# Twelve output stores of an attention and Fourier kernel, each in four pieces of 32 rows

## The chip, the cores and the metric

The kernel runs on one core of a Trainium2 chip. The metric is the device time of one execution in microseconds (us); lower is better. The engines are TensorE (PE; PEld are its weight loads), VectorE (DVE), ScalarE (ACT), GpSimd (POOL) and SyncE (SP), which here only issues transfers. ACT issues a few transfers too.

## The reference

The input is one sequence of 2048 tokens of 640 numbers in bf16. Two branches are mixed by a gate per token:

```
g = sigmoid((x * gate_w).sum(-1, keepdims=True))
a = attention(x, wq, wk, wv, wo, beta)      # 32 heads of 20, 4 segments of 512 tokens
b = irfft2(rfft2(B_x) * (w_r + 1j*w_i))     # over tokens and features
return g * a + (1 - g) * b
```

In each segment the attention is causal softmax attention within the segment. It is mixed per head, with sigmoid(beta), with a read of a memory: with phi(t) = t + 1 for positive t and exp(t) elsewhere, the read is phi(q) M / (phi(q) z + 1e-6). After a segment M and z grow by phi(k)^T v and by the sum of phi(k). The heads' outputs are then multiplied by wo. The first segment has an empty memory.

## The kernel before

The program is recorded as a list of operations with the buffers that each reads and writes, and then laid out by `Sched.schedule` (L111) in an order written out by hand as a list of numbers, `ORDER`. A number v stands for operation v // 2, on its first or second possible engine. Each engine runs its operations strictly in this order. `Sched.emit` (L249) puts in the waits: an operation waits for the last writer of what it reads and for the last users of what it overwrites.

A transfer is made by `Kern.dma` (L548 for a copy, L546 for a transposing load). Each gets one of 56 semaphores in turn and waits for the transfer that had the semaphore before; the bytes in flight are held under 1.6 MB. Nearly all transfers are issued by SP, one after another: an SP instruction that waits holds all that stand behind it.

Projections, attention and the Fourier transform fill PE through most of the program, interleaved. The end of a token's way is `finish_tile(s, a)` (L1506), for segment s and part a of it (four parts of 128 tokens):

- For the first three segments (s < 3) the attention's numerators come transposed from memory into `oU` (five loads, ld_u) and are multiplied by the reciprocal denominators `r4` (L1526, "normal"). The denominators go by way of memory: `rc` is stored into r_scr and loaded back as `r`.
- From the second segment on, the memory's part is loaded by a transposing load from o_scr into one of three buffers `mT`, and added to `oU` (L1534, "addmem").
- For each half of 320 columns PE sums in one PSUM bank the Fourier branch's last step ("Fb", L514, from `G` and the gate table `fbg`) and five products with wo ("oproj", L512). One copy to bf16, on ACT (L523) or DVE (L525), puts the half into one of four buffers `ot`.
- Then the finished 128 rows of 640 numbers, 160 KB, are stored from `ot`.

A row p = 32 q + j of `ot` holds token 512 s + 4 a + q + 16 j, so the four groups of 32 partitions are four token phases q. In the output these rows are 16 tokens apart. For s < 3 one transfer, st_out, stores the whole tile; its destination has the dimensions 4 phases, 32 tokens, 640 numbers. For the last segment (s = 3) four transfers, st_part, store a phase each, two issued by SP and two by ACT. The tile that reuses the `ot` buffer, four tiles later, waits until the stores out of it have landed.

In SP's order the first three st_out stand among the last loads of the third segment: after the store of `rc`; then come a key load `qkp` and a transposing load of `mT`; then the load of `r`; then two st_out; then two transposing loads of `mT`. The other nine stand behind these, the last eight with nothing but stores after them. At the very end SP waits for the semaphores of all output stores (L693), two to an instruction.

Of the kernel before, what the change touches and what calls it, by code (L numbers as in the profile page):

```python
# [12 lines left out]
P = 128  # L13
S = 2048
D = 640
# [3 lines left out]
L = 512  # L19
# [415 lines left out]
def dap(ap, off, *dims):  # L435
    return bass.AP(tensor=ap.tensor, offset=ap.offset + off, ap=[list(q) for q in dims])
# [25 lines left out]
class Kern:  # L462
# [10 lines left out]
    def b(self, *key):  # L473
        v = self.bufs.get(key)
        if v is None:
            v = self.bufs[key] = Buf(str(key))
        return v
# [64 lines left out]
    def dma(self, dst, src, nbytes, r, w, prio, tr=False, name="", after=(), queue="sp"):  # L542
# [16 lines left out]
        "ld_wka": (520.0, 1100.0, 16), "ld_wkb": (450.0, 2200.0, 16), "ld_wqa": (500.0, 1100.0, 16), "ld_wqb": (500.0, 2200.0, 16),  # L559
        "ld_wo": (600.0, 700.0, 16), "ld_wo2": (600.0, 3000.0, 16), "ld_wv": (450.0, 3000.0, 16), "ld_x": (450.0, 950.0, 16),  # L560
        "oT": (1300.0, 750.0, 16), "pad2": (370.0, 350.0, 10), "pad": (400.0, 1250.0, 10), ("pkT", 131072): (1260.0, 600.0, 16), ("pkT", 262144): (1280.0, 1100.0, 16),
        ("st_qk", 65536): (450.0, 220.0, 16), ("st_qk", 131072): (480.0, 350.0, 16), ("st_qk", 262144): (480.0, 720.0, 16), "st_g": (430.0, 150.0, 4), "st_o": (660.0, 950.0, 8), "st_out": (560.0, 1900.0, 4),
        "st_part": (430.0, 250.0, 16), "st_r": (480.0, 200.0, 16), "st_u": (520.0, 700.0, 16), ("xT", 131072): (1240.0, 1300.0, 16), ("xT", 262144): (1700.0, 2300.0, 16),
        ("xT", 393216): (1400.0, 2600.0, 16), ("xT", 655360): (2950.0, 2100.0, 16)}

    TSTART, TEND, F_START, F_END = 22.39, 193.27, 27.86, 215.71
# [75 lines left out]
        1564, 3542, 3072, 3544, 3129, 3088, 1568, 3546, 1603, 1570, 4012, 1529, 3122, 1573, 3138, 3432, 3148, 3125, 3548, 3552, 3194, 3150, 3564,  # L642
        3554, 1604, 3556, 3130, 3558, 3550, 3560, 1606, 3416, 1612, 3436, 3566, 3568, 3562, 3570, 1614, 3572, 3172, 3152, 3574, 3614, 3576, 3174,
        3438, 3578, 1608, 3580, 3440, 2562, 3442, 3583, 3444, 3196, 1574, 3616, 3446, 3618, 4034, 1577, 1610, 3156, 3176, 3620, 4016, 3622, 3158,
        1634, 3154, 4102, 3606, 3624, 1636, 3626, 1638, 3178, 3628, 3448, 3198, 3608, 3166, 1641, 1642, 3430, 3200, 1652, 3610, 3168, 1616, 1618,
        3612, 4030, 1620, 1644, 3170, 1654, 1623, 1646, 4028, 3654, 1656, 1648, 3160, 3184, 4042, 3584, 3656, 1658, 1650, 3162, 3670, 3250, 3658,
        3587, 1688, 3146, 3660, 3672, 1690, 2940, 1692, 3164, 3187, 1624, 1670, 1626, 4046, 1628, 4019, 1695, 3180, 2564, 1630, 3674, 1696, 1632,
        1698, 3182, 1700, 3214, 3202, 1702, 1660, 3216, 1678, 3188, 1672, 4036, 1680, 1674, 1662, 1704, 3462, 1664, 1682, 1676, 3588, 1666, 3206,
        3218, 4038, 1742, 1684, 3204, 3208, 1750, 4020, 1744, 1668, 1746, 3224, 1686, 3220, 1724, 1752, 1726, 4044, 1754, 1728, 1796, 3591, 3226,
        1748, 3230, 3222, 1730, 3598, 1756, 3232, 3464, 1798, 3210, 1800, 3600, 1732, 1758, 4080, 1734, 3228, 1736, 3602, 3238, 1803, 3470, 3212,  # L650
        3604, 3630, 1738, 3240, 3706, 3234, 3632, 3638, 1740, 3708, 1706, 3236, 3634, 1708, 3646, 3636, 1710, 4049, 4086, 3640, 3648, 3242, 1713,
        3710, 4090, 3650, 3642, 1778, 4023, 3652, 1780, 3244, 3688, 3644, 1714, 3690, 1716, 3246, 1782, 1804, 1718, 1806, 3692, 3694, 4024, 1808,
        1720, 1760, 3714, 4082, 1784, 1810, 3662, 4089, 1722, 4094, 1850, 3664, 1812, 3592, 1852, 1854, 3594, 1786, 3696, 3248, 1788, 1762, 1790,
        4040, 1858, 1860, 4222, 1862, 4032, 1764, 1856, 4092, 3748, 1766, 1792, 3678, 4206, 3750, 4208, 1864, 3666, 4210, 4098, 4212, 4214, 1794,
        1768, 3676, 4510, 1770, 1866, 1772, 4216, 4026, 4050, 3596, 4064, 4052, 4054, 4218, 3466, 3680, 1774, 3752, 1832, 4158, 3682, 1834, 3700,
        1836, 1776, 4056, 4066, 3754, 4068, 3252, 4070, 4072, 4058, 4150, 3668, 1840, 1842, 4074, 4154, 1838, 4084, 3756, 4076, 3698, 4146, 1844,
        3758, 3716, 1814, 1846, 1816, 4142, 3702, 3718, 3720, 3684, 1848, 4138, 3722, 3254, 3760, 4060, 4100, 3256, 4192, 4194, 3724, 3686, 4196,
        3726, 4062, 3774, 4096, 1818, 4078, 3776, 1886, 3728, 3762, 4198, 4200, 1820, 3468, 4202, 4104, 1888, 3778, 1822, 1824, 4224, 1826, 1890,
        3766, 3786, 1828, 4354, 4226, 3764, 1893, 3768, 4228, 4230, 3780, 1830, 4106, 4108, 4205, 4110, 3788, 4112, 4136, 4114, 4240, 3782, 4242,
        4116, 4220, 4232, 3790, 4234, 4119, 3792, 3784, 3802, 3794, 3804, 1894, 1896, 3704, 1898, 3806, 1900, 3808, 3770, 3796, 4244, 3772, 3810,  # L660
        4236, 1902, 4246, 4248, 4250, 4238, 3812, 3798, 3852, 3814, 4120, 3854, 4253, 3800, 4122, 4124, 1876, 4148, 4254, 3818, 3820, 4156, 1868,
        3822, 4140, 4256, 1870, 1872, 4144, 3824, 1874, 4152, 3928, 3712, 3826, 3732, 3828, 3930, 1878, 1880, 3734, 3736, 3830, 4160, 3856, 4320,
        3738, 4357, 4176, 3932, 3740, 4126, 4178, 3742, 4128, 4130, 3744, 4180, 4486, 3860, 4132, 4182, 3730, 3862, 1882, 3747, 4184, 4134, 4274,
        4358, 4360, 4362, 3864, 4186, 4258, 4364, 4366, 4368, 4189, 3866, 4418, 3920, 4370, 1884, 3858, 4490, 3922, 4276, 4322, 4260, 4372, 4262,
        3868, 4374, 4452, 4376, 4378, 4380, 4264, 4278, 4382, 4280, 4492, 4266, 3924, 4385, 3834, 4282, 3934, 3836, 4268, 4324, 4270, 4326, 3833,
        4162, 4273, 4328, 4284, 4330, 4164, 4287, 4166, 3870, 4168, 4332, 4170, 4288, 4334, 3816, 3842, 3838, 4336, 4402, 3844, 4404, 3872, 4406,
        4172, 4408, 3936, 4388, 4175, 4338, 4340, 3874, 4390, 4342, 4190, 4290, 3846, 4420, 4292, 4294, 4410, 3840, 4344, 4346, 4348, 3878, 3848,
        4351, 4296, 3880, 4392, 4412, 4352, 3850, 4394, 4298, 4415, 3888, 3876, 3890, 3892, 3894, 3882, 3884, 4304, 3896, 4396, 4300, 3898, 3886,
        4398, 4306, 4302, 4308, 3938, 4454, 4400, 3904, 4488, 3940, 3906, 4416, 3908, 3910, 3900, 3926, 4310, 4312, 3912, 4314, 4456, 3914, 4458,
        4317, 4470, 4472, 3942, 3946, 3916, 4318, 4460, 3948, 4436, 3902, 4474, 3944, 4462, 4464, 4438, 3950, 4466, 4440, 3952, 4442, 4469, 4476,  # L670
        4444, 3958, 4478, 4422, 3964, 3954, 3974, 3960, 3966, 4480, 4424, 4426, 3956, 4483, 4428, 4446, 4430, 4432, 4484, 3962, 3976, 3968, 3978,
        4435, 4386, 3970, 3980, 4448, 4498, 3972, 3982, 4494, 3984, 3990, 4450, 3992, 4496, 3986, 3994, 3996, 4500, 3989, 4548, 3998, 4526, 4512,
        4000, 4620, 3919, 4514, 4002, 4528, 4634, 4516, 4622, 4004, 4636, 4502, 4506, 4504, 4518, 4509, 4550, 4638, 4530, 4640, 4642, 4532, 4644,
        4552, 4534, 4647, 4520, 4624, 4522, 4536, 4626, 4525, 4628, 4538, 4562, 4564, 4566, 4568, 4546, 4540, 4630, 4570, 4554, 4633, 4542, 4544,
        4598, 4556, 4600, 4572, 4654, 4648, 4602, 4604, 4575, 4558, 4650, 4652, 4606, 4584, 4561, 4608, 4586, 4588, 4611, 4590, 4582, 4576, 4592,
        4594, 4578, 4580, 4597, 4614, 4616, 4618, 4612,
    )

    def texp(self, s, g, u=None):

# [3 lines left out]
    def build(self):  # L684
        nc = self.nc
        with nc.Block() as block:
            @block.gpsimd
            def _(pool):
                self.alloc()
                self.record()  # L690
                self.Sc.schedule(self.POOLS, self.ORDER)
                for s_, c in self.Sc.emit("st_out", "st_part"):
                    nc.sync.wait_ge(s_, c)  # L693

    def alloc(self):
# [810 lines left out]
    def finish_tile(self, s, a):  # L1506

        self.Sc.group += 1
        b = self.b
        prio = max(self.F_END + self.O_BASE + self.O_STEP * a, self.texp(s, 7, 4) + 4.0) if s < 3 else self.TEND + self.FIN[0] + self.FIN[1] * a  # L1510
        self.finc = getattr(self, "finc", -1) + 1
        k4 = self.finc % 4
        ot = self.ot[k4]
# [26 lines left out]
        otb = [b("ot", k4, hf) for hf in range(2)]  # L1540
        for hf in range(2):
# [14 lines left out]
            for c in range(5):  # L1556
# [5 lines left out]
                else:  # L1562
                    items = []
                    for q in range(4):
# [5 lines left out]
                self.mms(items, [b("oTl", c), b("wo2"), bank] if s == 3 else [ob[c], b("wo", c), bank], [], prio, name="oproj", mode=2 if s == 3 else -1)  # L1570
            self.Sc.op(self.copy_alts(lambda hf=hf: ot.ap(hf * 320, [1, 320]), lambda bank=bank: self.ps(bank, 0, [1, 320]), 320),
                       r=[bank], w=[otb[hf]], prio=prio, after=self.after_mid(("ot", k4, hf)), name="final")
        if s < 3:
            self.dma(lambda: dap(self.out, (s * L + 4 * a) * D, [D, 4], [16 * D, 32], [1, D]), lambda: ot.ap(0, [1, D]), P * D * 2, otb,
                     [b("out", s, a)], prio, name="st_out")
            return
        for q in range(4):
            self.dma(lambda q=q: dap(self.out, (s * L + 4 * a + q) * D, [16 * D, 32], [1, D]), lambda q=q: ot.ap(0, [1, D], p0=32 * q, np_=32),
                     32 * D * 2, otb, [b("out", s, a, q)], prio, name="st_part", queue=("sp", "act", "sp", "act")[q])

# [1 line left out]
_INS = ['A_x', 'A_wq', 'A_wk', 'A_wv', 'A_wo', 'A_beta', 'B_x', 'B_w_r', 'B_w_i', 'gate_w']  # L1582
# [24 lines left out]
```

## Time and profile before

| | |
|---|---|
| runs | 243.44, 241.42, 241.70 us; median 241.7 |
| profiled execution, its span (the page has no other time for it) | 245.4 us |
| PE, DVE, ACT, POOL busy | 228.8, 195.6, 199.9, 166.4 us |
| mean granted PE clock | 0.986 |
| output stores, 160 KB, from SP | 12 |
| output stores, 40 KB, from SP and from ACT | 8 and 8; 1.8 and 1.9 us to landing (median) |
| transposing loads of mT | 8; 5.5 us to landing (median) |
| SP's longest wait for a transfer after 180 us | 3.8 us, for r_scr |

The busy times are sums over the span and overlap. A transfer's time to landing runs from the start of its issue on SP to the last step of its semaphore. Times within the span count from its start.

### The profile page before, as it was taken

What the parts mean: (1) busy time and instruction counts of PE and PEld (TensorE: products, weight loads), DVE (VectorE), ACT (ScalarE), POOL (GpSimd) and SP (SyncE); (2) the same over time, 40 slices, a digit from 0 to 9 for tenths busy, and PEclk for the clock granted to TensorE, in tenths of its full rate; (3) what the DMA queues carried; (4) which work ended last, traced back from release to release, by engine and by line L of the source; (5) the groups of instructions that cost most, each with busy time, mean ns of one, the idle gap of its engine ahead of it and who ended that gap; (6) DMA issues with size and microseconds to landing.
All of it is one profiled execution on the core that took longest, in us unless ns stands there. A gap on an engine that the chain in (4) does not pass through costs nothing.

```text
span 245.4 us, 10243 instructions
## 1 busy us (share of the span) xinstructions
PE 228.8 (93%) x4347; PEld 140.8 (57%) x4361; DVE 195.6 (80%) x481; ACT 199.9 (81%) x241; POOL 166.4 (68%) x297
## 2 busy tenths in 40 slices
PE   7899999999999999999899999899999997699994
PEld 2574567765455665545556555465454565366794
DVE  0479998889999987989999898989889867435563
ACT  2289698988999999999899889999999976388740
POOL 8513268557969846768947998859898694359730
PEclk9999999999999999999999999999999999589999
DMA  7999959975799875575698661375758997812123
GB/s 168 278 365 208 239 160 178 318 140 164 210 200 174 168 226 143 125 199 135 202 233 234 185 186 53 99 210 146 222 151 194 230 140 96 127 36 85 57 84 108
DMA packets 58928, 42.17 MB, mean 172 GB/s; under 512 B 30020, under 2 KB 55172, under 8 KB 58884
## 3 DMA queue, kind: packets, MB, share of 16 engines
q1 hardware_dynamic: 57844, 40.96, 69.2%
q8 instruction: 34, 0.56, 1.0%
q10 hardware_dynamic: 1040, 0.57, 0.8%
q14 instruction: 10, 0.08, 0.1%
HBM read 23.32 MB, written 12.30 MB: 145 GB/s over the span
## 4 chain that ended last, share of the span: by engine, by line
PE 54%; DVE 18%; ACT 12%; DMA 10%; issue 3%; SPq 1%; DVEq 0%
PE psum L514 48%; ACT ex L1263 9%; PE psum L512 6%; DMA pkn<-phk 4%; DMA r_scr<-rc 3%; DMA xT<-in_A_x_dram 2%; DVE xsb L906 2%; DVE Pt L1439 2%; DVE xf L901 1%; DVE phk L1085 1%; ACT et L1072 1%; DVE oU L1526 1%; DVE G L1485 1%; DVE ub L525 1%; DVE va L1115 1%
## 5 line engine op out<-in xcount | busy, mean ns | idle before, releaser
L1263 ACT ACTIVATE ex<-psum 128x2048 bf16<-128x2048 f32 (+4 forms) x92 | 138.7, 1507 | 16.3 <-PE psum L514 14.3
L1284 POOL TENSOR_SCALAR_AFFINE_SELECT ex<-ex 128x256 bf16<-128x256 bf16 (+2 forms) x224 | 122.1, 567 | 42.0 <-ACT ex L1263 38.4
L514 PE MATMUL psum<-qkp 20*64 20x64 bf16 (+5 forms) x1280 | 32.7, 271 | 4.8 <-issue 2.3
L514 PE MATMUL psum<-xT,wk 128*128 128x256 bf16 (+1 forms) x280 | 34.0, 273 | 0.9 <-DMA wk<-in_A_wk_dram 0.6
L514 PE MATMUL psum<-wv,xT 128*32 128x321 bf16 (+3 forms) x400 | 30.0, 301 | 0.6 <-DVE va L1115 0.3
L514 PE MATMUL psum<-xT,wq 128*128 128x512 bf16 (+1 forms) x121 | 27.0, 380 | 1.3 <-DMA xT<-in_A_x_dram 0.7
L1439 DVE TENSOR_TENSOR Pt<-psum,Wt 128x642 bf16<-128x642 f32 x32 | 25.5, 820 | 2.3 <-PE psum L514 1.9
L514 PEld LDWEIGHTS psum<-qkp 20*64 20x64 bf16 x1280 | 13.4, 103 | 19.5 <-ACT ex L1263 13.2
L514 PEld LDWEIGHTS psum<-xT,wk 128*128 128x128 bf16 (+1 forms) x280 | 19.9, 97 | 7.0 <-DMA wk<-in_A_wk_dram 1.1
L512 PE MATMUL psum<-wo,oU 128*32 128x320 bf16 x480 | 23.4, 313 | 0.5 <-DVE oU L1534 0.5
L906 POOL TENSOR_TENSOR xsb<-xf 128x320 bf16<-128x320 bf16 (+2 forms) x12 | 9.2, 763 | 17.1 <-DVE xsb L906 13.2
L525 DVE CAST ot<-psum 128x320 bf16<-128x320 f32 x21 | 10.1, 491 | 12.9 <-PE psum L512 10.5
L514 PEld LDWEIGHTS psum<-wv,xT 128*32 128x32 bf16 (+1 forms) x400 | 14.3, 96 | 8.3 <-issue 2.4
L514 PE MATMUL psum<-big,Ac 128*128 128x160 bf16 (+2 forms) x96 | 18.1, 258 | 0.7 <-DVE Pt L1439 0.3
L1115 DVE TENSOR_TENSOR va<-psum,ebx 128x320 bf16<-128x320 f32 x32 | 15.2, 483 | 4.2 <-ACT gate L1113 2.1
L514 PE MATMUL psum<-big,Cp 128*128 128x321 bf16 (+1 forms) x96 | 18.0, 302 | 0.2 <-DVE G L1485 0.2
L514 PE MATMUL psum<-ex,va 128*32 128x64 bf16 (+3 forms) x576 | 17.4, 256 | 0.7 <-DVE dn L1152 0.3
L1485 DVE TENSOR_TENSOR G<-eo,psum 128x320 bf16<-128x320 f32 x32 | 14.7, 482 | 3.9 <-PE psum L514 2.8
L512 PEld LDWEIGHTS psum<-wo,oU 128*32 128x32 bf16 x480 | 12.4, 100 | 8.8 <-issue 4.2
L514 PE MATMUL psum<-tt,Yt 128*128 128x256 bf16 (+1 forms) x96 | 16.5, 275 | 0.3
L514 PEld LDWEIGHTS psum<-ex,va 128*32 128x32 bf16 x576 | 11.1, 96 | 9.7 <-POOL ex L1284 3.4
L1072 ACT ACTIVATE et<-qu 128x512 bf16<-128x512 bf16 x25 | 15.6, 630 | 0.2
(99 smaller groups left out, 391.9 us busy)
## 6 DMA issues: line engine op xcount, KB each, us to landing
qkp<-qk_scr SPq DMA_DIRECT2D x28, 160.0 KB
tt<-tab_tt SPq DMA_DIRECT2D x8, 512.0 KB, 4.3
qk_scr<-qu SPq DMA_DIRECT2D x12, 256.0 KB, 3.1
u_scr<-ub SPq DMA_DIRECT2D x12, 256.0 KB, 3.9
xsb<-in_A_x_dram SPq DMA_DIRECT2D x8, 320.0 KB, 6.8
oU<-u_scr SPq DMA_DIRECT2D x15, 128.0 KB, 2.9
out_dram<-ot SPq DMA_DIRECT2D x12, 160.0 KB
Wt<-in_B_w_r_dram SPq DMA_DIRECT2D x16, 80.2 KB, 2.6
```

The source lines that it names most:

```text
L512: h = e.matmul(dst, wt, r_, start=st, stop=sp_, **{**kw, "tile_position": (0, q), "skip_group_check": True})
L514: h = e.matmul(o_, l_, r_, start=st, stop=sp_, **kw)
L525: alts["dve"] = (lambda e: e.tensor_copy(dst(), src()), 67 + 1.04 * n, 68.0)
L901: self.either(lambda e, r=r, op=op: e.tensor_tensor(xf.ap(r * 642, [321, 2], [1, 320]), xs.ap(o, [D, 2], [1, 320]), xs.ap(o + 320, [D, 2], ...
L906: self.either(lambda e, dst=dst, src=src, d0=d0, n=n, op=op: e.tensor_tensor(xs.ap(o + dst, [D, 2], [1, n]), xf.ap(src + d0, [321, 2], [1, ...
L1072: self.one("act", lambda e: e.activation(et.ap(0, [1, L]), qsl(), ACT.Exp), L, [qb], [b("et", pi_)], late, name="phi_exp")
L1085: fmin = lambda e: e.tensor_tensor(dst(), dst(), et.ap(0, [1, L]), ALU.min)
L1115: self.one("dve", lambda e: e.tensor_tensor(va.ap(i * H * VW + h0 * VW, [VW, nh], [1, DH]), self.ps(bank, 0, [DH, nh], [1, DH]), self.ebx. ...
L1263: self.one("act", lambda e, d=d, q=q: e.activation(self.ex.ap(*d), self.ps(bank, *q), ACT.Exp, scale=SC), n, [bank], [self.exb(s, 2 * pr + ...
L1284: self.one("pool", lambda e: e.affine_select(self.ex.ap(e0 + d0, [1280, 4], [1, n], np_=np_), self.ex.ap(e0 + s0, [1280, 4], [1, n], np_=np_),
L1439: self.one("dve", lambda e, ri=ri, Pt=Pt, Wt=Wt, wo_=wo_, bank=bank: e.tensor_tensor(Pt.ap(ri * 322, [644, 2], [1, KD]), self.ps(bank, 0, ...
L1485: self.one("dve", lambda e, q=q, n2=n2, bank=bank, eo=eo: e.tensor_tensor(self.G.ap(n2 * D + 639 * q, [1 - 2 * q, 320]), eo.ap(q, [1, 320] ...
```

## The change

The twelve st_out become 48 st_part of 32 rows and 40 KB each, one for each token phase. All four of a tile are issued by SP, in the place in SP's order that the one store had. Nothing else in any engine's order changes. The reuse of an `ot` buffer now waits for four transfers where it waited for one, semaphores are handed out to 36 transfers more, and SP's wait at the end covers them all.

```
         "st_g": (430.0, 150.0, 4), "st_o": (660.0, 950.0, 8),
-        "st_out": (560.0, 1900.0, 4),
         "st_part": (430.0, 250.0, 16),
...
-    ORDER = ( ..., 4102, ... )
+    ORDER = ( ..., 4108, ... )          # renumbered; 4 numbers in place of one at each store, e.g. 4078, 4080, 4082, 4084
...
-                for s_, c in self.Sc.emit("st_out", "st_part"):
+                for s_, c in self.Sc.emit("st_part"):
                     nc.sync.wait_ge(s_, c)
...
-        if s < 3:
-            self.dma(lambda: dap(self.out, (s * L + 4 * a) * D, [D, 4], [16 * D, 32], [1, D]), lambda: ot.ap(0, [1, D]), P * D * 2, otb,
-                     [b("out", s, a)], prio, name="st_out")
-            return
         for q in range(4):
             self.dma(lambda q=q: dap(self.out, (s * L + 4 * a + q) * D, [16 * D, 32], [1, D]), lambda q=q: ot.ap(0, [1, D], p0=32 * q, np_=32),
-                     32 * D * 2, otb, [b("out", s, a, q)], prio, name="st_part", queue=("sp", "act", "sp", "act")[q])
+                     32 * D * 2, otb, [b("out", s, a, q)], prio, name="st_part", queue=("sp", "act", "sp", "act")[q] if s == 3 else "sp")
```

## The prediction

> **What bounds the kernel now.** The page came first, for the stages in which TensorE (PE) is not full. Its 40 slices last 6.1 us each.
>
> ```profile
> span 245.4 us, 10243 instructions
> PE   7899999999999999999899999899999997699994
> PEclk9999999999999999999999999999999999589999
> DMA  7999959975799875575698661375758997812123
> ```
>
> PE is full except in two slices, 202 to 215 us, where the transfers are busy and the PE clock then falls. Next the chain that ended last, for that stretch:
>
> ```profile
> 194.85 6.89 DMA r_scr<-rc
> ...
> 208.81 0.24 PE psum L514 x15
> 209.06 2.35 issue
> 211.41 0.21 PE psum L514
> ```
>
> From 211.41 to the end the chain is PE and one last eviction, so what PE loses here is lost at the end. Then SyncE's queue (SP) and VectorE (DVE) there; columns are start, length, engine:
>
> ```profile
> 195.50 0.64 SPq L548 DMA_DIRECT2D out_dram<-ot  x1
> 196.18 0.50 SPq L548 DMA_DIRECT2D qkp<-qk_scr  x1
> 196.73 1.23 SPq L546 DMA_TRANSPOSE mT<-o_scr  x1
> 201.76 0.56 SPq L548 DMA_DIRECT2D r<-r_scr  x1
> 202.42 1.31 SPq L548 DMA_DIRECT2D out_dram<-ot  x2
> 203.79 5.47 SPq L546 DMA_TRANSPOSE mT<-o_scr  x2
> ...
> 211.01 0.49 DVE L1534 TENSOR_TENSOR oU<-oU,mT 128x640 bf16<-128x640 bf16 x1 [1.45 <-DMA mT<-o_scr]
> ```
>
> Three stores that change (195.50, 202.42, 203.15) stand just ahead of transposing loads of mT. The load issued at 203.79 takes 7.2 us to land, and DVE waits for it:
>
> ```profile
> DMA to landing us min/median/max: 7.2/7.2/7.2
> ```
>
> Why so long: the trace keeps every step of a transfer's semaphore. A 160 KB store shows one step at once and four late ones: it runs on four of the 16 DMA engines, and undisturbed (219.90) lands 3.8 us after issue. The stores of 202.42 and 203.15 finish at 207.05 and 208.80; the transpose's packets begin at 205.6 on free engines, all hang for 2.6 to 3.0 us and end together at 208.65. It lands at 209.3 to 209.5 on 15 engines and 210.99 on the last. The same happens at 201.46 and 214.97, each after a store. The load at 215.02, with no store ahead, lands in 2.8 us.
>
> The 2.35 us "issue" has no semaphore behind it. PE's code comes as 34 packets of 16 KB. One begins at 201.58 and one at 208.76, right after two of the hangs; PE stops at its instruction 6,835 (0.51 us from 203.61) and at 7,091 (209.06), 256 apart, and goes on 1.5 us after each packet ends. So in this execution PE ran out of code, which the held transfers delayed. The clock by stage:
>
> ```profile
> core 0: us, PE busy (x) PEld busy (x) DVE busy (x) ACT busy (x) POOL busy (x), PEclk, DMA share, GB/s
> 202.59:209.42 6.83, 5.13 (x157) 3.61 (x150) 5.28 (x15) 4.55 (x5) 2.92 (x4) 1.00 0.69 94
> 209.42:216.25 6.83, 4.84 (x73) 2.45 (x76) 1.92 (x5) 2.79 (x4) 1.89 (x4) 0.50 0.79 112
> 216.25:223.07 6.82, 6.82 (x208) 4.50 (x208) 2.60 (x6) 5.51 (x6) 5.41 (x10) 1.00 0.21 50
> ```
>
> After a stretch with PE 75% busy the clock was halved for 6.83 us; 4.71 us of PE work fell into it, which costs 2.35 us.
>
> **This execution and the runs.** The span, 245.4, is 3.7 us above the median of 241.7 so this execution lost something that the usual run keeps. Take out both code stops and the half clock (0.51 + 2.35 + 2.35 = 5.2) and put in their place the wait that they hide: with code at hand PE passes 209.06 and does 40 matmuls of 0.14 us per four (1.4) and twelve attention matmuls (0.25), to 210.7; its next transposes wait for a DVE copy that follows the mT addition, 211.01 + 0.49 + 0.49 = 212.0. That is 1.3 us. 245.4 - 5.2 + 1.3 = 241.5, where two of three runs lie. I take it that the usual run has the 1.3 us wait and not the starving.
>
> **The change, part by part.**
>
> *SP's issues.* 12 stores become 48 pieces. The final 40 KB pieces, on the same queue, price them:
>
> ```profile
> L548 SPq DMA_DIRECT2D out_dram<-ot x8: 314/424/576, 239.6 to 243.2; - x8
> DMA to landing us min/median/max: 1.5/1.8/2.0
> ```
>
> With a gap of 0.05 a piece is 0.47 and a group of four 1.88, against 0.68 for the whole store: +1.2 us on SP each time. The bounds are 0.36 and 0.63 a piece; the median serves. First store: the key load qkp goes from 196.18 to 197.4 and mT to 197.9; behind them SP waits from 197.96 to 201.76 for r_scr, which is ahead of the pieces, so 3.8 us of wait hide 1.2. Without that cover, the r load and all behind it would be 1.2 later. qkp landed at 201.60, behind the store on its engines, for PE's use at 201.78; one issued with little ahead (107.62) takes 2.8, so now 200.2; at its 5.4 of before it would be 202.8 and PE 1.0 late, ahead of its later waits. Second and third: mT's load goes from 203.79 to 202.42 + 3.76 = 206.2 (205.3 to 207.5). The next load waits for its buffer until 208.06 anyway. The 210.36 store puts the load of 211.58 to 212.3, for a use at 221.7. From 219.90 on SP has 1.8 to 3.5 us per store; the last three (232.24 on) would end at 237.9, before the final pieces at 239.58.
>
> *The transfers.* A store's 2.8 us on four engines become about 0.7 on each of 16, so nothing is left to hang on. I take the 2.8 us of the free load (215.02) for mT: 206.2 + 2.8 = 209.0. The other end is the 4.1 us of the load at 211.58, behind a store: 210.3.
>
> *DVE and PE.* The addition comes after a DVE operation that ends at 209.56, so at 209.6 instead of 211.01; its copy is done by 210.6, and PE, arriving at 210.7, does not wait. Gain 1.3, or 0.6 at the late landing. As PE's code is held no longer, the starving goes where it happens: PE reaches the transposes of 214.92 at 210.7 (-4.2), or, at half clock from 209.42 on, at 209.42 + 2 x 1.29 = 212.0 (-2.9).
>
> *Waits.* An eviction into a reused ot buffer waits for four semaphores, not one. Wait instructions carry two each and are 61 ns apart at SP's end, so this is at most 0.12 on an engine that idled 0.2 to 2.6 us for PE before most of these evictions. The first store's pieces should land by 199.2 for an eviction at 201.57; were they as late as r_scr's last step (201.74, plus 0.7), ScalarE would lose 0.9, of which its idle 0.5 at 204.72 hides half. Behind the eviction stand exponentials that PE needs. SP's closing waits go from 14 to 26 instructions: 243.69 + 25 x 0.061 = 245.22 against 245.16, +0.06.
>
> Sum for the usual run: 241.7 - 1.3 + 0.06 = 240.5; with a gain of 0.6 it is 241.2, and with half of the starving's 2.35 us still in the usual run and gone, 239.3.
>
> *Rules against it.* The Trainium skill, "DMA: Bandwidth & Descriptors", section "Rules for kernel authors", advises one 128-partition transfer over partial ones and says small transfers under 64 KB are mostly overhead; its fit under "Anatomy of one DMA" would land 160 KB in about 2.4 us (an estimate from its figures), so that splitting only makes SP later, and the sum would be a loss of about 2.4 us less what waits hide. The trace has 3.8 and up for the whole store and 1.8 for a piece, so the row decides here. On the clock, "TensorE: Matmul & The Clock Gate", Part 1, has it fall after an idle window of about 3.4 us; the longest stop here is 2.35, so by the page there was nothing to lose, while the row shows the loss.
>
> **The rivals.**
>
> *B: the usual run starves too,* and the profiled one is slow for another reason. For it: the order of transfers is the same in every run, and one run took 243.44. Against: the agreement at 241.5 above. Then 2.9 to 4.2 us go: 237.5 to 238.8.
>
> *C: hidden.* The landing is no better than about 210.8, because one engine is held by a code packet (1.2 us, as the last step at 210.99 was), or PE waits for something else, or the pieces do not spread. Against the last: all final pieces show 16 separate steps. Landing at 210.8 gains 0.2, so 241.5; with the 0.4 that ScalarE could lose as above, and the 0.06, 242.2.
>
> *D: slower.* SP becomes what mT waits for. At 0.63 a piece the load is issued at 207.5, and with the 5.5 us that mT takes by the median of the page it lands at 213.0 instead of 210.99: 241.7 + 2.0 = 243.7, and 246.0 if the longer stop also halves the clock for 4.7 us. It decides from where issue plus landing passes 210.99, that is from a landing of 4.8 us at 206.2. For it: SP is a strict queue, and eight issues stand ahead of the load. Against: the long landings all stood behind stores or a full queue.
>
> **How the numbers follow.** A (as summed) 0.50, B 0.22, C 0.16, D 0.12. About 1%, 2.4 us, is what a measurement of this kernel tells from no change. Below 239.3 lie B and the lower end of A: 0.25. Above 244.1 lies the upper half of D: 0.07. The rest, 0.68, is within 1%. The forecast is A's 240.5, with 239.3 to 241.2 as its own range. The range of 237.6 to 242.7 takes A, C and nearly all of B, and leaves out D and B's best end, some 0.15.
>
> **What would show it.** In the changed profile: no 256-byte packets that hang for over 1 us after 195 us; SP's pieces 0.4 to 0.5 apart; mT's load issued near 206.2 and landed near 209; DVE's addition without a wait on mT, near 209.6; no "issue" of over 0.5 us in the chain after 200; SP's wait for r_scr still there. Wrong it would be if DVE still waited for mT, now because of SP; if the pieces took over 0.6 each; or if PE stood at the same place with the transfers idle, for then its code was not held by the stores.

## The result and the profile after

The kernel with the pieces is slower by 0.6%: 244.03 us against 242.97 us (medians of 20 runs each on one chip), ratio 1.0061, 95% interval 1.0033 to 1.009. The ratio leaves out three executions that lie more than 1.5% above the fastest of their kernel (two of the unchanged kernel, 245.49 and 248.08, and one of the changed, 246.75); without them the median of the unchanged kernel is 242.6. The profiled execution took 243.51 us with a span of 241.5. Where the time of a profiled execution is known, it is its span plus 2.0 us (1.8 to 2.4 over all kernels here). The profile of before that the prediction read (span 245.4) thus shows a run of about 247.4 us (an estimate), far above the median. A second profile of the unchanged kernel (first experiment below: span 239.7, a run of 241.73 us) is what the profile after is compared with here.

The page of the changed kernel, as it was read for before, and under it the PE line of that second profile:

```profile
span 241.5 us, 10306 instructions
PE   7799999999999999999899999899989999998894
PEclk9999999999999999999999999999999999999998
DMA  7999859995996885393789572364865976572223
...
PE   7799999999999999999999999899999999899994
```

Against the profile that the prediction read, the dip of slices 34 and 35 and the fall of the clock are gone, but the second profile of the unchanged kernel does not have them either (its 8 in slice 35 is a wait of 0.5 us at 206 us, which the changed kernel has too, and a stop of 0.3 us). New are the 8s in slices 37 and 38, 217 to 229 us. SyncE's queue (SP) in the stage of the mT loads; columns are start, length, engine, line and operation:

```profile
194.40 2.62 SPq L548 DMA_DIRECT2D out_dram<-ot  x4
197.07 0.36 SPq L548 DMA_DIRECT2D qkp<-qk_scr  x1
197.47 1.23 SPq L546 DMA_TRANSPOSE mT<-o_scr  x1
198.75 0.59 SPq L548 DMA_DIRECT2D r<-r_scr  x1
199.43 5.73 SPq L548 DMA_DIRECT2D out_dram<-ot  x8
205.21 2.64 SPq L546 DMA_TRANSPOSE mT<-o_scr  x2
...
214.91 18.91 SPq L548 DMA_DIRECT2D out_dram<-ot  x32
```

Four pieces take 2.5 to 2.9 us of SP here, not 1.88, and from 214.91 on SP issues the 32 pieces of the last eight tiles almost without a pause: 18.91 us, of which 0.9 us are waits for two copies, so 2.25 us a tile. The load of mT that the prediction followed is the first of the two at 205.21; it landed at 208.07. VectorE (DVE) takes this load within 0.03 us of its landing, in the unchanged kernel:

```profile
208.05 0.50 DVE L1534 TENSOR_TENSOR oU<-oU,mT 128x640 bf16<-128x640 bf16 x1
```

and in the changed one:

```profile
208.10 0.65 DVE L1533 TENSOR_TENSOR oU<-oU,mT 128x640 bf16<-128x640 bf16 x1
```

In the unchanged kernel this load went out at 202.73, hung behind the 160 KB stores until 207.15 and landed at 208.02. So the pieces did shorten its way from 5.3 to 2.9 us, and SP's longer way ate it up; nothing waited for it for more than 0.1 us before, and nothing does now. The next load of mT is another matter. Issued at 206.65, it landed at 211.04, and DVE waited for it in the changed kernel, where the unchanged one took it at 209.83 without a wait:

```profile
211.06 0.49 DVE L1533 TENSOR_TENSOR oU<-oU,mT 128x640 bf16<-128x640 bf16 x1 [1.41 <-DMA mT<-o_scr]
```

That wait cost PE nothing: PE is busy all through it, as the second row of the next view shows.

The clock by stage, core 0 of the changed kernel (columns: PE, PEld, DVE, ACT, POOL busy, granted PE clock, DMA share, GB/s):

```profile
202.71:209.54 6.83, 6.29 (x198) 4.37 (x194) 6.68 (x17) 5.43 (x8) 4.09 (x6) 1.00 0.39 82
209.54:216.37 6.83, 6.83 (x200) 4.68 (x202) 3.46 (x8) 6.37 (x7) 5.34 (x11) 1.00 0.75 113
216.37:223.20 6.83, 5.83 (x188) 4.09 (x180) 3.87 (x10) 4.50 (x6) 3.78 (x7) 1.00 0.28 70
```

PE is full where it stood before, and loses 1.0 us in the stage behind it. The chain of waits names the place (steps of "issue" and of queues of up to 0.05 us between these are left out):

```profile
217.03 0.50 DVE ot L525
217.53 0.88 SPq L548
218.45 0.42 SPq L548
218.92 0.42 SPq L548
219.38 1.60 DMA out_dram<-ot
221.09 0.78 ACT ot L523 x2
221.88 1.36 SPq L548
...
225.62 1.49 SPq L548
227.15 1.61 DMA out_dram<-ot
228.88 0.50 DVE ot L525
229.43 8.77 PE psum L514 x244
238.21 0.49 DVE ot L525
```

A copy fills an ot buffer, SP issues the pieces out of it one after another, the last lands 1.6 us after its issue, and only then may the next copy into that buffer begin; PE waits behind that copy. The two PE gaps are 219.22 to 219.96 and 228.78 to 229.43, in sum 1.39 us of the 1.8 by which this span is longer than the 239.7. In the unchanged kernel the same stretch is PE alone:

```profile
226.66 9.82 PE psum L514 x284
236.48 0.02 issue
236.51 0.49 DVE ot L525
```

What ended the idle time ahead of the ot copies and stores after 196 us (us, times), in the changed kernel:

```profile
  PE psum L512: 5.7, 9
  PE psum L514: 5.6, 8
  DMA out_dram<-ot: 3.5, 2
```

in the second profile of the unchanged kernel and in the one that the prediction read:

```profile
  DMA out_dram<-ot: 1.3, 2
...
  DMA out_dram<-ot: 0.4, 1
```

That last line was there to be seen: already with whole stores a copy waited for its buffer.

One more thing on SP's issues. A piece's issue takes 0.42 us as a rule, but nine times after 195 us one takes 1.0 to 1.6 (the 1.49 us of the one at 216.92 begin with a wait of 0.6 for its copy; the chain has the 0.88 after it). Each of these falls together with a packet of PE's code, and ends 0.35 to 0.38 us after it: packets that end at 218.04, 222.88 and 226.74, issues that end at 218.41, 223.24 and 227.10. Pieces issued just ahead of such a packet land 2.7 to 3.7 us after their issue in place of 1.6. The whole stores in the tail of the unchanged kernel take 0.54 to 0.56 to issue, packet or not.

### The profile page after: what moved, and what is told of

Read it like the earlier page. It is cut to its first block, busy times and chain, and to the rows that moved or that the text cites. A ratio compares the mean times of both kernels' runs of the same rounds, so it can differ in the third digit from the quotient of the medians.

```text
span 241.5 us, 10306 instructions
## 1 busy us (share of the span) xinstructions
PE 226.3 (94%) x4347; PEld 140.1 (58%) x4361; DVE 197.5 (82%) x481; ACT 199.5 (83%) x241; POOL 166.3 (69%) x297
## 4 chain that ended last, share of the span: by engine, by line
PE 53%; DVE 17%; ACT 13%; DMA 6%; SPq 6%; issue 3%; DVEq 0%; ACTq 0%
PE psum L514 49%; ACT ex L1262 9%; PE psum L512 5%; SPq L548 4%; DMA xsb<-in_A_x_dram 3%; DVE xf L900 2%; DMA pkn<-phk 2%; DVE xsb L905 2%; SPq L546 2%; DMA out_dram<-ot 1%; ACT et L1071 1%; DVE ub L525 1%; DVE oU L1525 1%; DVE va L1114 1%; DVE phk L1084 1%
## 5 line engine op out<-in xcount | busy, mean ns | idle before, releaser
L512 PE MATMUL psum<-wo,oU 128*32 128x320 bf16 x480 | 21.9, 300 | 0.5 <-DVE oU L1533 0.5
```

The lines of the kernel that those rows point to most:

```text
L512: h = e.matmul(dst, wt, r_, start=st, stop=sp_, **{**kw, "tile_position": (0, q), "skip_group_check": True})
```

## The experiments

Theory S: SP's issues in the tail hold the ot buffers. Its rivals change from step to step, as the expectations say. Times are medians in us.

**1. The unchanged kernel again.**

```
(no edit)
```

> The kernel before, unchanged, for a second profile of it. If the first profile was an outlier (it lies 3.7 us over the median), this span is 239 to 241.5 us, PE has no stop of over 0.5 us without a cause after 200 us and the clock is not halved; only a wait of about 1 us that goes back to the transposing load of mT is left. If the usual run starves for code too, the 2.35 us stop is there again. The ratio of the times is 1.000 within 0.004 either way.

Measured: 242.89, ratio 1.000 [0.9971, 1.003]; span 239.7. It has no half clock and no wait for mT of over 0.1 us (shown above). Of the stop of 2.35 us 0.27 us is left, at the same instruction 7,091 (207.45). Its copies waited 1.3 us for ot. This profiled run is faster than the median of its twelve by 1.2 us, so what the slower ones wait for is not shown.

**2 and 3. The two halves of the change.**

```
-        if s < 3:
+        if s < 3 and (s, a) not in [(0, 0), (0, 1), (1, 0), (1, 1)]:     # 2: the first four in SP's order in pieces, eight whole
+        if s < 3 and (s, a) not in [the other eight]:                    # 3: the last eight in pieces, four whole
```

> Only the four stores that stand ahead of transposing loads are in pieces, the last eight are whole. Theory S (the loss comes from SP, whose 48 issues set the pace after 215 us, so that copies wait for their ot buffer): the tail is that of before and mT's load is no longer held, so 0.6 to 1.3 us faster than before, ratio 0.995 to 0.998, and SP's issues after 215 us are as far apart as before. Rival R (pieces on all 16 engines hold up other transfers wherever they are): not faster than before, ratio 1.000 to 1.004.

> Only the last eight stores, with nothing but stores behind them on SP, are in pieces. Theory S: all of the loss and none of the gain, 1.5 to 2.7 us slower, ratio 1.006 to 1.011, with copies that wait for out_dram<-ot after 215 us. Rival R: two thirds of the changed kernel's loss of 1.5 us, ratio 1.003 to 1.005.

Measured: the first four in pieces 242.9, 0.9999 [0.9967, 1.003]; the last eight in pieces 243.49, 1.0012 [0.9981, 1.0044]. Neither half shows a loss that stands out. For the second this is a miss for S, whose 1.006 to 1.011 lies above the interval. Single runs of the second spread from 241.6 to 244.8, with one at 249.8, which hides a difference of 1 us. The gain for the first four that S expected (0.995 to 0.998) isn't there either.

**4. All in pieces, with six ot buffers.** The two more lie where `ub` was.

```
-        k4 = self.finc % 4
+        k4 = (0, 1, 5, 3, 4, 2, 1, 3, 0, 4, 2, 5, 0, 1, 4, 3)[self.finc]     # of six
```

> All twelve stores in pieces, as in the changed kernel, but with six ot buffers in place of four (the two more lie where the numerators' staging has ended). Theory S: SP is as late as before but nobody waits for it; the copies' waits for out_dram<-ot fall from about 1.4 us on PE to under 0.3, ratio to before 0.994 to 1.000. Rival R: the buffers do not matter, ratio 1.005 to 1.008 like the changed kernel.

Measured: 243.08, 1.0009 [0.9978, 1.004], and no copy waited for ot. Theory R's 1.005 to 1.008 is outside. The loss is smaller than the 1.0061 of the change itself, though the intervals overlap. Theory S's 0.994 to 1.000 lies mostly within the interval. No run has whole stores and six buffers with the transposing loads, and the changed kernel was measured in one job only.

**5 to 8. The same with less noise.** In the next runs the transposing loads are plain ones, so nothing is transposed and the output is not the reference's. That takes away the stage that the prediction was about, leaves the tail with its stores and PE code as it was, and shrinks the spread of the whole stores: they then run at 239.78 to 240.70. The pieces still spread over 3.0 us.

```
-                return e.dma_start_transpose(d_, s_)
+                (rp, rows), (cp, cols) = s_.ap[0], s_.ap[-1]
+                s_ = bass.AP(tensor=s_.tensor, offset=s_.offset, ap=[[rp * rows // 128, 128], [rp, rows // 128], [cp, cols]])
```

> The kernel before with its 23 transposing loads replaced by plain loads of the same bytes into the same buffers, so what is computed is not the reference's. After 215 us the kernel before has only stores and PE's code on its DMA engines, so the tail (the last eight tiles) should run as it did; earlier stages may be shorter. It is the base for the three runs that follow. Ratio to before 0.97 to 1.00. Theory S: its copies wait 0.5 to 1.5 us for their ot buffers, as in the repeated run of before.

> The changed kernel (12 stores in 48 pieces), again with plain loads in place of the transposing ones. Theory S (SyncE's issues in the tail hold the ot buffers): 1.0 to 2.2 us longer than the plain kernel with whole stores, 0.4 to 0.9% of it; copies wait 2 to 4 us for ot; SyncE issues without pause from about the second tile of the last eight on. Theory M (the loss lies in the stage of the mT loads): without transposing loads it is gone, the two within 0.2%, or the pieces are faster.

Measured: whole stores 240.15 (0.9874 of before, [0.9833, 0.9916]), pieces 241.73 (0.9941 [0.9904, 0.9978]). The pieces cost 1.6 us, and ten of their twelve runs lie above the slowest with whole stores. The loss is there without one transposing load, so theory M falls. In the whole stores' profile one copy waited 0.4 us for ot, just under S's 0.5 to 1.5.

The third was to keep a piece on four DMA engines:

```
-  dap(self.out, (s * L + 4 * a + q) * D, [16 * D, 32], [1, D])
+  dap(self.out, (s * L + 4 * a + q) * D, [128 * D, 4], [16 * D, 8], [1, D])     # s < 3
```

> As the one before, but the destination of each of the 48 pieces has an outer dimension of four, so that each piece runs on four DMA engines as the whole store did. The number of issues stays, the spreading over 16 engines goes. Theory S by count (0.47 us an issue): the same loss as the 48 pieces on 16 engines, 1.0 to 2.2 us over the plain kernel with whole stores. Theory S by holding (an issue that meets a PE code packet takes 1.1 to 1.6 us): no issue over 0.8 us, and at most half of that loss, 0 to 0.8 us.

Measured: 241.74, 0.9952 [0.9916, 0.9987]. The edit did not do what it should: each piece still shows 16 semaphore steps (8 rows of 16 * D are 128 * D, so the two dimensions are together the old one of 32). So it decides nothing between the two forms of S, but repeats the plain pieces, with the same +1.6 us. Its chain shows the price without a fall of the clock:

```profile
214.44 0.50 DVE ot L525
...
215.32 0.42 SPq L549
215.74 0.04 issue
215.78 1.90 SPq L549
217.68 0.04 issue
217.73 1.60 DMA out_dram<-ot
...
219.44 0.45 ACT ot L523
...
223.66 1.70 SPq L549
225.36 0.04 issue
225.41 1.60 DMA out_dram<-ot
...
227.12 0.50 DVE ot L525
227.63 0.05 issue
227.67 8.77 PE psum L514 x244
```

The 1.90 and the 1.70 are issues that met PE's code. They took 1.5 and 1.3 us more than the usual 0.42; by that much earlier, as an estimate, the pieces would have released both buffers.

The fourth gave half of the pieces to ScalarE (ACT):

```
-  queue=("sp", "act", "sp", "act")[q] if s == 3 else "sp")
+  queue=("sp", "act", "sp", "act")[q])
```

> As the plain kernel in 48 pieces on 16 engines, but two pieces of each of the 12 tiles are issued by ACT in place of SyncE, in the same places of the order, as the last four tiles have it. Theory S: SyncE then spends about 0.94 us on a tile, the waits for ot fall to those of whole stores, and what is left is ACT's own issue time, about 0.9 us a tile, of which its idle time ahead of the copies (0.6 to 2 us for most tiles) hides most: within -0.3% to +0.3% of the plain kernel with whole stores. If SyncE is not the price: 0.4 to 0.9% slower than whole stores, as the pieces from SyncE, or worse by ACT's 0.9 us a tile.

Measured: 245.44, 1.0103 [1.0049, 1.0157], 5.3 us over whole stores. This is a miss, and the worst of all. ACT's issues meet PE's code too, and ACT's exponentials, which PE waits for, stand behind them. The chain, at the first store and in the tail:

```profile
193.04 0.38 ACTq L549
193.45 0.74 ACTq L549
194.24 0.60 ACT ex L1263
...
223.40 0.44 ACTq L549
223.89 0.61 ACT ex L1263
```

PE stood 0.9 us from 194.80 there. The profiled run is the fastest of its six (243.63), so it does not show all of the 5.3 us; the three slowest have a mean clock of 0.986 to 0.993, the others 1.000.

**9 to 12. Issue count, width, and place.** All with plain loads.

```
  # 9: the whole store, and behind it, from the same ot
+            for q in range(3):
+                self.dma(lambda q=q: dap(self.td.ap(), (12 * s + 3 * a + q) * D, [D, 1], [1, D]), lambda q=q: ot.ap(0, [1, D], p0=32 * q, np_=1), ...)
  # 10: pieces with their rows in another order
+  dap(self.out, (s * L + 4 * a + q) * D, [16 * D, 4], [64 * D, 8], [1, D])       # s < 3
  # 11, 12: as 3 and 2
```

> The plain kernel with whole stores, and behind each of the 12 stores three stores of one row (1,280 bytes) each out of the same ot buffer into a scratch tensor that nothing reads: 48 issues from SyncE in the places of the 48 pieces, but hardly a byte more, and nothing spread over 16 engines. Theory S by count (the number of issues is the price): 1.0 to 2.2 us longer than the plain kernel with whole stores, about as the plain pieces (+1.6). Theory S by holding (a piece's issue is held while a PE code packet blocks one of its 16 engines): no issue over 0.8 us but for chance, and -0.3 to +0.6 us.

> The plain kernel in 48 pieces, the rows of each written in another order, so that the destination's dimensions of 4 and 8 rows can't be merged into one of 32 (in the run before they were: it showed 16 steps a piece). If this puts a piece on four engines, its semaphore shows four or five steps. Theory S by holding: then no issue over 0.8 us unless the code's engine is among the four, and at most half of the loss of the pieces, 0 to 0.8 us over plain whole stores. Theory S by count: 1.0 to 2.2 us over them. If it shows 16 steps again, it repeats the plain pieces: +1.2 to +2.0 us.

> Plain loads; the last eight stores in pieces, the first four whole. Theory S: the loss lies here, 0.8 to 1.8 us over plain whole stores, with waits for ot of 2 us or more, since only the last eight stand close together. If only all twelve together cost, through a backlog on SyncE that the fourth brings along: -0.3 to +0.6 us.

> Plain loads; the first four stores in pieces, the last eight whole. Theory S: SyncE has the time for them, -0.4 to +0.5 us against plain whole stores. If the loss is in the stage of the loads (SyncE's issues ahead of the mT and key loads): +0.8 to +1.6 us.

Measured: three tiny stores more 242.01 (0.9958 [0.9936, 0.998]), rows permuted 242.57 (0.9996 [0.9973, 1.0019]), last eight in pieces 241.44 (0.9954 [0.9926, 0.9982]), first four in pieces 240.16 (0.9885 [0.9863, 0.9907]). Against 240.15 that is +1.9, +2.4, +1.3 and 0.0 us. These four and the two of 13 and 14 ran on other chips than 5 to 8; by the ratios to the unchanged kernel of each job the four are +2.0, +3.0, +1.9 and +0.3, each uncertain by about 1 us. Either way, the loss lies with the last eight. With the rows permuted (they land in other places of the output) a piece does run on four engines (four or five steps), and no issue is held. But each costs more of SP:

```profile
L549 SPq DMA_DIRECT2D out_dram<-ot x32: 615/616/622, 213.2 to 233.8; - x32
```

(ns min/median/max.) Theory S by holding expected at most 0.8 us here and 0.6 us for the tiny stores, and missed both. By count, S has the tiny stores in its range of 1.0 to 2.2 us and the permuted pieces just above it. These runs do not tell what part the count and what part the hold has in the pieces. What all the slower ones have in common is the time from a full buffer to a free one. Here it is for the fifth of the last eight tiles, whose buffer the copies at about 227 us want; ends of the last copy into it, last landing out of it, and start of the copy that reuses it, from each trace. The column "PE tail" is the time from the end of PE's wait at about 206 us to its last matmul:

| kernel | filled | landed | reused | filled to landed | PE tail | median over plain whole |
|---|---|---|---|---|---|---|
| whole stores (1) | 222.92 | 226.75 | 226.84 | 3.83 | 29.98 | |
| changed | 223.81 | 228.75 | 228.86 | 4.94 | 31.49 | |
| last eight in pieces (3) | 222.47 | 227.15 | 227.25 | 4.68 | 30.24 | |
| plain, whole (5) | 221.42 | 225.24 | 225.33 | 3.82 | 29.53 | 0 |
| plain, first four in pieces (12) | 221.88 | 225.68 | 225.77 | 3.80 | 29.53 | 0.0 |
| plain, whole and three tiny (9) | 223.04 | 227.44 | 227.57 | 4.40 | 30.93 | +1.9 |
| plain, pieces, dimensions merged (7) | 222.16 | 227.00 | 227.11 | 4.84 | 30.56 | +1.6 |
| plain, pieces (6) | 222.40 | 227.30 | 227.41 | 4.90 | 31.90, 1.7 of it by a half clock | +1.6 |
| plain, last eight in pieces (11) | 223.44 | 228.70 | 228.80 | 5.26 | 32.28, 1.7 of it by a half clock | +1.3 |
| plain, rows permuted (10) | 222.99 | 228.13 | 228.23 | 5.14 | 31.47 | +2.4 |

In every one the reuse begins about 0.1 us after the landing, with whole stores too: the copies of the kernel before had no slack at this place. PE had some: its tail takes the same 29.53 us in runs 5 and 12, where one copy waits 0.4 us, as in the runs with six buffers (4, 13 and 14), where none waits. Wherever the last eight tiles have pieces or tiny stores and four buffers, the tail takes 0.7 to 2.0 us more, the half clock apart. That is the price in PE's time, and between run 1 and the changed kernel it is the 1.5 us of the ratio. Whole stores can have it too: run 2, whose last eight are whole, takes 30.87, as two of them, issued at 216.00 and 217.03, land after 4.5 and 5.1 us. A whole store lands 3.8 us after its buffer is full. Pieces land 1.6 us after the last issue, which is 2.9 us after the buffer is full if SP is free (213.56 to 216.47 in run 6), but 4.8 to 5.3 when SP is behind or an issue is held. One profile each is too little to read the order of the medians off the tails; the sign is the same in all.

**13 and 14. Six buffers, with plain loads.**

> The plain kernel in 48 pieces with six ot buffers in place of four (the two more lie where ub0 and ub1 were). SyncE's 48 issues and their packets stay, only the copies have the buffers of two more tiles. If the reuse of ot is the whole price of the pieces: no wait for ot, and -0.3 to +0.4 us against plain whole stores with four buffers (240.15 us), that is 1.2 to 1.9 us better than the plain pieces (241.73 us). If SyncE's lateness or the packets cost elsewhere too: +0.8 us or more.

> The plain kernel with whole stores and six ot buffers, the control for the run before, and the only candidate that these runs leave for a gain. Its copies wait 0.4 us for ot with four buffers, not on the chain: -0.4 to +0.2 us against plain whole stores with four buffers (240.15 us).

Measured: pieces 241.53 (0.9955 [0.9925, 0.9984]), whole stores 240.46 (0.9912 [0.9878, 0.9945]). No copy waits for ot in either, and from the end of PE's wait at 206 us to the start of the last copy the two spend the same time (29.58 and 29.59 us). Yet the pieces are 1.1 us slower, so S as I put it missed: the reuse of ot is not the whole price. The rest is at the very end. With pieces the span goes on for 3.23 us after the last copy, with whole stores for 2.60; in run 4 it is 3.3, in run 1 2.7. SP is still busy with pieces when the final stores become due: its last piece is issued from 232.45 to 233.76 (held by a code packet), and SP's first final store, which ACT's counterpart preceded at 232.92, follows at 233.86. That is 0.6 of the 1.1 us. Where the other 0.5 is, these two profiles do not show; they differ by 0.3 us ahead of 206 us, which may be chance. Run 14, with +0.3, lies just above its -0.4 to +0.2, within the noise. No run beat whole stores in four buffers.

## Why the prediction was wrong

**The usual run.** The step "I take it that the usual run has the 1.3 us wait and not the starving" failed. It was built by subtracting from a span of 245.4 what looked unusual, down to a run time of 241.5, as if span and run time were one. They differ by 2.0 us, so the spans of the three runs were about 239.4 to 241.4, and the sum left no room for a wait. The repeated run has none: DVE takes mT at 208.05, 0.03 us after it landed, and PE is busy. Term of 1.3 us: measured nothing there. Rival B gets no support either, as the repeated run stops for 0.27 us there and not 2.35. The base of the sum was off too: 241.7 is the median of three runs; that of twenty is 242.97, which by itself lies above the range of 237.6 to 242.7.

**SP in the tail.** This is the step that gives the loss. I had written that "From 219.90 on SP has 1.8 to 3.5 us per store" and compared that with 1.88 us of issues. The question was not whether SP gets done in time for the end, but when each buffer comes free: 4.94 us after it is full in place of 3.83. And 1.88 was mis-sized, by pricing pieces at the median of the eight final ones (0.42 an issue): in the tail, where some are held, four pieces cost 2.25. This term was costed at nothing and measured +1.5 us of 244 by the ratio, and 1.5 us in PE's tail (31.49 for 29.98).

**Waits of the copies.** I costed only the wait instructions ("at most 0.12"), and named as cover the idle time of 0.2 to 2.6 us for PE that most copies have. One of them in the tail had none: its line (0.4, 1) said that it waited for out_dram. In the changed kernel two wait, 3.5 us in all.

**Right as far as it went.** mT's issue (206.2 forecast, 205.21 measured), its landing (209.0 and 208.07), its way of 2.8 us (2.9), no "issue" of over 0.5 us in the chain after 200, and no stop of PE with the transfers idle. Pieces are mostly 0.46 apart, as said, but for those that PE's code held. DVE's addition has no wait on the mT load that the prediction followed, but the sign of being wrong that it named, DVE waiting for mT because of SP, came with the next load (1.41 us, at no cost to PE). Hanging 256-byte packets did not go away altogether: up to 1.58 us at 199.4 to 201.0. SP's wait for r_scr, said to stay, was gone: that store landed at 197.93, ahead of SP.

**Rival D** had the sign and the time (243.7 to 246.0) from the wrong place: SP did become what PE waits for, but by way of ot, not of mT. That its time holds the 244.03 is luck, since its base is the same 241.7.

**The rule against it.** The Trainium skill, "DMA: Bandwidth & Descriptors", "Rules for kernel authors", advises one large transfer in place of several under 64 KB. The prediction set it aside, since a piece lands in 1.6 to 1.8 us and a whole store in 3.8. Both rows stand, and the rule still had it right here, through the issue time of SP: 2.25 us a tile for 0.54. The fit under "Anatomy of one DMA", which the prediction used for its 2.4 us, is the page's for transfers that GpSimd issues; these come from SP.

## What to carry to other kernels

When a transfer out of a reused buffer is split, follow the buffer: from the last write into it over all issues to the last landing, and set that beside the moment at which the next writer is ready. A shorter transfer does not help if the issues that precede its last part take longer than what it saves, and a copy that begins 0.1 us after a landing has no slack left, even if the line says only 0.4 us of waiting. Before building on one profile, set its span, plus what lies around it, beside the spread of the runs; and if an issue queue has no pause left, more buffers can carry its lateness to the end, as in runs 4 and 13.

## What the runs showed of the hardware

- An SP or ACT issue of a 40 KB piece on 16 engines that began while a 16 KB packet of PE's code was under way was in most cases held to 0.35 to 0.38 us after the packet's end (up to 1.9 us in place of 0.42). Not always: SP's first final store in the changed kernel, at 235.46 in the packet of 235.18 to 236.45, took 0.31 us, and the next one was held to 236.81. Transfers on four engines were not held in the tail: 0.54 to 0.56 us for whole stores, 0.62 for the permuted pieces.
- A piece on four engines costs SP 0.62 us, one on sixteen 0.42. The Trainium skill, "DMA: Bandwidth & Descriptors", "Why a DMA increments its semaphore by 16 and not by 1", says that a copy on fewer engines than its increment takes an extra write by the sequencer; the rows agree in direction, and no run here shows the cause.
- The clock fell to half for 3.41 us, 1.3 us after a PE gap of 0.59 us, in the plain pieces (run 6):

```profile
222.19:229.02 6.83, 6.24 (x209) 4.67 (x202) 3.14 (x9) 4.32 (x8) 5.32 (x11) 1.00 0.27 70
229.02:235.85 6.83, 6.83 (x150) 5.36 (x150) 2.91 (x7) 1.51 (x3) 1.41 (x2) 0.75 0.20 51
```

A clock of 0.75 over 6.83 us is 1.7 us of PE work lost. This profiled run (243.61) is the slowest of its twelve, and the three slowest are the three with a mean clock of 0.993; with whole stores (runs 5, 9, 12 and 14) none of the 25 runs up to 242.2 us has a mean under 0.999. But the gap alone does not decide it: in the changed kernel PE had two gaps of that size and kept its clock, and in run 11 the clock fell after a gap of 0.52 us at 205.3 that runs 5 and 12 have too, without a fall. So a short wait costs its own length in one run and 1.7 us more in another; what decides is not shown.
